# One table of instruction order exchanged for another, and the unread keys left unturned, in a fused attention and gated-MLP kernel

## The chip, the cores and the metric

The kernel runs on one core of a Trainium2 chip. The metric is device time in microseconds (us) of one execution; several executions are timed and their median is quoted. A profile is one execution recorded by the hardware profiler; its times count from the first instruction of the span.

## The reference

```python
B, H, S, D = 4, 8, 768, 48
for t in range(S):                                   # per batch and head
    state = alpha[t][:, None] * state + outer(k[t], v[t])
    y[t] = q[t] @ state
x = y.transpose(0, 2, 1, 3).reshape(3072, 384)
g = x @ w_gate                                       # 384 x 1536
out = ((g * sigmoid(g)) * (x @ w_val)) @ w_out       # 1536 x 384
```

All arrays are float32 (the weights arrive as float64 words and are reduced to single precision on the chip).

## The kernel before

**Tiling.** The recurrence is cut into 16 units: four batches of 768 tokens by four units of 192 tokens, each of three chunks of 64. Unit u of a batch is the last one where u is 3, 7, 11 or 15. Two units make one block of 384 rows for the MLP, so there are 8 blocks. The hidden width of 1536 is cut into 12 slices, and a step is one block and one slice: 96 steps, numbered in the order in which the program takes them (blocks 0 and 1 are taken in halves of 7 and 5 slices, the others whole).

**One step s** is a chain of words. `g` and `v` are nine matmuls each on TensorE (a value and its rounding remainder make three products per K tile), `sl` is SiLU on ScalarE, `h` the product with `v` on VectorE, `hh` the rounded copy on ScalarE, `hl` the remainder on VectorE or GpSimd, `o` nine matmuls into three accumulators. There is one PSUM bank for `g` (gps) and one for `v` (vps), so the next `v` waits for `h` of the step before, and the next `g` for its `sl`.

**One unit u.** `La`, `Lk`, `Lq` and `V` load alpha, keys, queries and values from SyncE (SP); the first four units are widened (`pa`, `pk`, `pq`) and turned by TensorE (`Ta`, `Tk`, `Tq`, evacuated by `ea`, `ek`, `cq`), the others are turned by VectorE (`tr`, `tk`, `tq`). `G` and `f` are the backward and forward scans, 1.8 us each on VectorE; `mk` and `q` multiply keys and queries by them, `qc` copies half of the queries. The keys are turned once more into the tile K: for the first four units by TensorE (`K`, copied by `kc`), for the others by VectorE (`kr`, lines 529 to 543: sixteen transposes a unit, each over all three chunks). `S` or a burst `Z` (from unit 4 on: outputs of unit u-1, scores and carried state of unit u in one run of small matmuls) use them; `ma` masks the scores, `ad` adds the carried state, `yh` and `yl` split the outputs, `xr` moves them by DMA (line 745) into the rows of xT that `g` and `v` read. The state that the last unit of a batch would carry past its third chunk is not computed (line 578), so its third chunk of K is not read.

**Weights.** `wl` loads a group, `w..v0` to `w..v2` cut it to single precision, `w..a` rounds it, `w..p` takes the remainder. `wr`/`wc` and `Lc`/`ck` load weights and alpha again for a range check, `fl` sums the verdicts (lines 828 to 839), `ot`/`os` take and store the outputs, `pl` loads a stored partial sum.

**Order.** Nothing schedules the program at build time but the table `ORDER` (line 44): each entry is an engine's letter (t TensorE, v VectorE, s ScalarE, g GpSimd, y SP) and a word, with the numbers of PSUM banks after an @. Each engine runs its words strictly in the order of the table; between engines only data and buffers order them. All loads and all `xr` are issued by SP, in order. The DMAs of the built program use eight semaphores in turn.

Of the kernel before, what the change touches and what calls it, by code (L numbers as in the profile page):

```python
# [49 lines left out]
t:Y0@36 s:yh0.0 y:La3 t:Ta2@20 s:pa3 s:ea2 y:Lk2 y:V1.0 s:w1a s:yh0.1 g:w1p y:Lq2 y:V1.3 y:V1.5 y:V1.2 v:w3v2 v:de1  # L50
t:S1@71 t:C1.0@2 s:ad1.0 v:yl0.0 v:ma1.2 t:Ta3@15 t:C1.1@4 s:ad1.1 t:C1.2@0 y:wl4 s:w4v0 s:ad1.2 g:pq2 g:pk2 g:vc1
v:ma1.1 v:yl0.1 v:ma1.0 t:Y1@64 s:yh1.0 v:w2v2 v:w2a s:yh1.1 t:R0.1@0 t:R0.2@3 t:Tq2@72 s:x0.2 s:x0.1 s:cq2 v:G2
v:yl1.0 v:yl1.1 t:R1.1@6 s:x1.1 v:w4v1 v:w4v2 t:Tk2@74 v:mk2 v:f2 v:q2 y:Lk3 s:pk3 t:R1.0@0 t:R0.0@6 y:V2.4 s:x0.0
s:x1.0 t:R1.2@7 s:x1.2 t:K2.0@2 s:kc2.0 g:w2p y:wl5 s:w5v0 y:V2.2 y:V2.0 y:Lq3 g:pq3 s:w4a t:Tk3@34 t:K2.1@7 s:kc2.1
t:g0 s:sl0 y:V3.1 y:V2.1 y:wl7 y:V2.3 y:V2.5 v:de2 g:vc2 g:lm0 y:V3.2 y:wl8 y:wl6 y:V3.3 y:V3.0 v:w5v1 s:ea3 v:G3
t:S2@20 s:qc2 v:ma2.2 v:mk3 v:ma2.0 v:lm1 y:wl11 y:wl9 y:V3.4 y:V3.5 s:w3a g:w3p g:w4p v:ma2.1 t:C2.0@7 t:K2.2@1
s:kc2.2 s:ad2.0 t:g1 t:v0 t:C2.1@3 v:h0 s:ad2.1 s:sl1 t:K3.0@7 s:kc3.0 t:Tq3@03 t:C2.2@1 s:ad2.2 s:cq3 s:hh0 s:w6v0
v:f3 t:v1 t:K3.1@7 t:g2 v:w5v2 g:hl0 v:h1 v:q3 v:de3 v:w6v1 s:hh1 s:kc3.1 s:sl2 t:Y2@20 s:yh2.0 v:hl1 v:w6v2 t:C3.0@4
t:S3@67 s:w5a g:w5p t:v2 s:ad3.0 t:C3.1@1 s:yh2.1 v:ma3.2 v:w8v0 v:yl2.0 s:w6a g:w6p t:o0 t:o1 v:ma3.1 v:yl2.1 y:wl12
y:La4 y:V4.5 y:wl10 s:w7v0 s:qc3 v:h2 v:ma3.0 y:xr2.0 y:xr2.1 v:w7v1 v:w7v2 v:w8v1 s:w9v0 s:ad3.1 s:vc3 t:g3 v:w8v2  # L60
v:w9v1 y:Lk4 y:wl13 y:xr2.2 t:Y3@20 s:sl3 s:w7a s:hh2 v:hl2 v:w7p s:w8a v:w8p s:yh3.0 s:yh3.1 t:v3 v:h3 s:w10v0 v:w9v2
s:hh3 v:hl3 t:g4 v:w10v1 s:sl4 s:w9a g:w9p t:o2 t:v4 v:yl3.1 v:yl3.0 v:h4 s:hh4 g:hl4 t:g5 v:w10v2 v:w10a s:w11v0
s:sl5 s:w12v0 t:v5 t:o3 v:w11v1 v:w10p t:g6 s:sl6 v:w12v1 v:w11v2 s:w11a v:h5 g:w11p s:hh5 t:o4 g:hl5 v:w12v2 y:xr3.0
y:xr3.1 y:xr3.2 y:wl16 y:V4.1 y:wl14 t:v6 v:tk4 v:h6 s:hh6 g:hl6 t:g7 v:tr4 v:G4 s:sl7 s:w13v0 s:w12a y:Lq4 v:mk4
# [1101 lines left out]
```

## Time and profile before

| what | value |
|---|---|
| timed runs | 550.12 us median (550.12, 547.42, 550.28) |
| profiled execution | span 548.1 us; its own device time is not listed beside the span |
| TensorE busy (PE) | 528.0 us, 96% of the span |
| VectorE busy (DVE) | 400.5 us, 73% |
| ScalarE busy (ACT) | 249.4 us, 45% |
| GpSimd busy (POOL) | 151.2 us, 28% |
| granted TensorE clock | 0.999 mean |
| DMA moved | 77.61 MB, 142 GB/s mean |

The busy time of an engine is the union of its instructions. SPq is the queue of SP, which only issues. An arrow in square brackets names what ended the idle time before an instruction. Matmul ends are modelled and overlap the next start, so the length of a run of matmuls is read from start to start.

### The profile page before, as it was taken

How to read it: one execution, taken by the hardware profiler on the slowest of the kernel's cores; microseconds unless marked ns; L12 is line 12 of the kernel's file. 1: busy time of each engine (PE TensorE's matmuls, PEld its weight loads, DVE VectorE, ACT ScalarE, POOL GpSimd, SP SyncE). 2: the span in 40 equal slices, each digit the busy share in tenths (PEclk: the TensorE clock that was granted, in tenths of full speed). 3: DMA queues.
4: the chain of work that ended last, by engine and by line, in shares of the span. 5: the costliest groups of instructions: out<-in, count | busy, mean ns of one | idle time of the engine just before them, and what ended most of it. 6: DMA issues, size and time to landing. Idle time of an engine off the chain costs nothing.

```text
span 548.1 us, 13557 instructions
## 1 busy us (share of the span) xinstructions
PE 528.0 (96%) x5350; PEld 513.7 (94%) x5350; DVE 400.5 (73%) x755; ACT 249.4 (45%) x578; POOL 151.2 (28%) x149
## 2 busy tenths in 40 slices
...
GB/s 243 256 263 292 146 173 249 107 139 174 85 187 151 141 106 185 157 120 73 169 76 101 203 158 112 76 136 129 184 153 73 90 50 158 135 58 104 155 50 47
DMA packets 96195, 77.61 MB, mean 142 GB/s; under 512 B 33280, under 2 KB 93056, under 8 KB 96128
## 3 DMA queue, kind: packets, MB, share of 16 engines
...
## 4 chain that ended last, share of the span: by engine, by line
PE 66%; DVE 3%; DMA 2%; SPq 1%; issue 1%; ACT 0%; POOL 0%; DVEq 0%; POOLq 0%
PE v L760 20%; PE ops L793 20%; PE g L760 20%; PE c L680 2%; PE s L565 1%; DMA L<-in_q_dram 1%; PE c L584 1%; PE y L658 1%; PE y L659 1%; DMA xT<-X 1%; SPq L745 1%; DMA V<-in_v_dram 1%; DVE h L772 0%; DVE V L629 0%; DVE K L540 0%
## 5 line engine op out<-in xcount | busy, mean ns | idle before, releaser
L760 PE MATMUL v<-xT,w 128*128 128x384 f32 x864 | 167.3, 337 | 0.6 <-DMA xT<-X 0.6
L760 PE MATMUL g<-xT,w 128*128 128x384 f32 x864 | 166.6, 336 | 0.6 <-ACT h L768 0.4
L793 PE MATMUL ops<-w,hh 128*128 128x384 f32 x576 | 158.5, 336 | 0.0
L760 PEld LDWEIGHTS v<-xT,w 128*128 128x128 f32 x864 | 150.5, 188 | 2.2 <-issue 0.9
L760 PEld LDWEIGHTS g<-xT,w 128*128 128x128 f32 x864 | 150.7, 188 | 1.8 <-ACT h L768 0.9
L781 POOL TENSOR_TENSOR hl<-h,hh 128x384 fp32r<-128x384 f32 x65 | 69.8, 1075 | 285.5 <-ACT hh L776 271.8
L772 DVE TENSOR_TENSOR h<-h,v 128x384 f32<-128x384 f32 x96 | 53.0, 552 | 89.9 <-PE v L760 61.6
L793 PEld LDWEIGHTS ops<-w,hh 128*128 128x128 f32 x576 | 105.5, 188 | 0.3
L768 ACT ACTIVATE h<-g 128x384 f32<-128x384 f32 x96 | 47.1, 490 | 119.6 <-PE g L760 101.0
L776 ACT CAST hh<-h 128x384 fp32r<-128x384 f32 x96 | 49.1, 511 | 112.0 <-DVE h L772 77.4
L793 PE MATMUL ops<-w,hl 128*128 128x384 f32 x288 | 96.8, 336 | 0.0
L540 DVE STREAM_TRANSPOSE K<-Gs 32x192 f32<-32x192 f32 x192 | 71.1, 370 | 3.3
L793 PEld LDWEIGHTS ops<-w,hl 128*128 128x128 f32 x288 | 54.0, 188 | 0.0
L347 POOL TENSOR_TENSOR w<-t,w 128x768 fp32r<-128x768 f32 (+1 forms) x15 | 27.5, 1842 | 34.4 <-ACT w L343 25.3
L781 DVE TENSOR_TENSOR hl<-h,hh 128x384 fp32r<-128x384 f32 x31 | 18.4, 594 | 22.8 <-ACT hh L776 22.7
L481 DVE TENSOR_TENSOR_SCAN AT<-AT,back 128x771 f32<-128x771 f32 x16 | 29.2, 1824 | 0.6
L606 DVE TENSOR_TENSOR X<-s,mask 64x384 f32<-64x384 f32 (+1 forms) x48 | 26.3, 551 | 3.8 <-PE s L565 3.1
L472 DVE TENSOR_TENSOR_SCAN Gs<-AT,inj 128x772 f32<-128x772 f32 x16 | 28.5, 1780 | 0.5 <-ACT AT L866 0.3
L497 POOL TENSOR_TENSOR X<-trq,AT 112x768 f32<-112x768 f32 x11 | 18.7, 1703 | 32.1 <-DMA xT<-X 11.0
L320 ACT ACTIVATE wc<-wc,wbias 128x384 f32<-128x384 f32 x36 | 23.3, 648 | 1.2
L629 DVE TENSOR_TENSOR V<-c,V 48x96 f32<-48x96 f32 x84 | 21.4, 255 | 2.8 <-ACT V L627 0.5
L893 POOL TENSOR_TENSOR Gs<-trk,Gs 128x768 f32<-128x768 f32 x9 | 15.3, 1700 | 26.0 <-DVE Gs L472 22.2
(120 smaller groups left out, 525.8 us busy)
## 6 DMA issues: line engine op xcount, KB each, us to landing
...
```

Of the source, the lines that this page charges most:

```text
L320: nc.scalar.activation(dev, dev, AF.Relu, bias=wbias, scale=-1.0, accum_out=wviol[:, 0, i : i + 1])
L347: eng.tensor_tensor(out=lo, in0=src, in1=hi.bitcast(F32), op=ALU.subtract)
L472: nc.vector.tensor_tensor_scan(*(x.rearrange("p g t -> p (g t)")[:, ::-1] for x in (Gs, AT, inj)), 0.0, op0=ALU.mult, op1=ALU.add)
L481: nc.vector.tensor_tensor_scan(Af, Af, back[:, 1 : n + 1], back[:, 0:1], op0=ALU.mult, op1=ALU.add)
L540: nc.vector.transpose(out=bass.AP(k0.tensor, k0.offset, [k0.ap[0], (G * 2 * D, NU), (2 * D, GF), (1, 32)]), in_=Kg[j * BO + x : j * BO + x ...
L606: nc.vector.tensor_tensor(out=X[r, z, f * GF : (f + 1) * GF, :].rearrange("r g (c t) -> r g c t", c=NU), in0=sps[f][r].rearrange("r g (c t ...
L760: nc.tensor.matmul(pt, wsp[kind, f][a][:, kt * P : (kt + 1) * P], xT[blk][:, b_, kt, :], start=(n == 0), stop=(n == 3 * KT - 1),)
L768: nc.scalar.activation(h, acc.pop(("g", blk, f)), AF.Silu)
L772: nc.vector.tensor_tensor(out=h, in0=h, in1=acc.pop(("v", blk, f)), op=ALU.mult)
L776: nc.scalar.copy(out=hh, in_=acc["h", blk, f])
L781: eng.tensor_tensor(out=hl, in0=acc.pop(("h", blk, f)), in1=hh.bitcast(F32), op=ALU.subtract)
L793: nc.tensor.matmul(ops[blk][i], h[b_][:, i * P : (i + 1) * P], wsp["o", f][a], start=(first and n == 0), stop=(last and n == 2),)
```

## The change

Two things are exchanged. The table `ORDER` is a different permutation of the same words: the order on each engine, the engine of some words (below) and most PSUM banks of the attention's early matmuls differ. And the third chunk of K is not turned where it is not read: `K3.2` and `kc3.2` (four TensorE transposes, two ScalarE copies) are dropped, and `kr` of units 7, 11 and 15 turns two chunks of three (48 VectorE transposes, 128 elements a row in place of 192).

Words by engine, before and after: `hl` GpSimd 65 to 61, VectorE 31 to 35; `q` GpSimd 11 to 8, VectorE 5 to 8; `qc` GpSimd 7 to 5, ScalarE 9 to 6, VectorE 0 to 5; `pq` GpSimd 3 to 0, ScalarE 1 to 3, VectorE 0 to 1; `pa` VectorE 1 to 0, ScalarE 3 to 4; weight rounding `w..a` ScalarE 18 to 15, VectorE 2 to 0, GpSimd 0 to 5; `ot` ScalarE 15 to 14, VectorE 15 to 16.

```diff
@@ ORDER: first and last lines of either table
-s:first y:La0 s:pa0 t:Ta0@23 s:ea0 y:wl0 y:Lq0 s:pq0 v:w0v0 v:w0v1 v:w0v2 v:G0 v:f0 t:Tq0@03 v:q0 y:La1 s:pa1 t:Ta1@72
-s:w0a v:w0p y:Lk1 s:pk1 y:Lk0 s:pk0 y:wl1 s:w1v0 t:Tk1@14 y:Lq1 t:Tk0@05 g:pq1 y:V0.2 y:V0.3 y:V0.1 v:w1v1 v:mk0 s:ea1
...
-s:hh92 s:wc24 v:hl92 s:sl94 t:v94 v:h94 t:o91 t:g93 y:Lc9 y:Lc13 s:sl93 t:v93 t:o92 v:h93 s:hh94 s:ck13 s:ck9 v:fl
-s:hh93 g:hl94 g:hl93 t:v95 t:g95 s:sl95 t:o93 t:o94 v:h95 s:hh95 v:hl95 t:o95 t:cp@2 v:ot95.0 y:os95.0 v:ot95.1
-s:ot95.2 y:os95.1 s:oz0 y:oz1 v:fg
+s:first y:La0 s:pa0 y:wl0 y:Lq0 y:La1 t:Ta0@65 v:w0v0 v:w0v1 y:Lk1 s:ea0 v:pq0 v:w0v2 s:pa1 t:Tq0@13 s:pk1 t:Ta1@42
+y:Lk0 v:G0 s:pk0 g:w0a t:Tk1@70 t:Tk0@56 y:V0.0 v:f0 v:q0 s:ek1 v:mk0 s:ea1 y:La2 y:V0.2 g:w0p y:Lq1 y:V1.3 y:V0.1
...
+v:h94 g:hl92 t:g93 t:o91 s:hh94 s:sl93 t:o92 t:v93 v:h93 t:g95 t:v95 s:hh93 s:wc24 v:hl93 s:sl95 s:wc33 t:o93 v:hl94
+v:h95 v:fl t:o94 s:hh95 v:hl95 t:o95 s:ot95.1 s:ot95.2 s:oz0 v:ot95.0 y:os95.0 t:cp@6 y:os95.1 y:oz1 v:fg
@@ k_rows
         k_tile(u)
-        Kg = state[u]["Gs"][:, :, 1:].rearrange("r g (c t) -> r c g t", c=NU)
+        nc_ = NU - last_of_batch(u)
+        Kg = state[u]["Gs"][:, :, 1:].rearrange("r g (c t) -> r c g t", c=NU)[:, 0:nc_]
...
-                    out=bass.AP(k0.tensor, k0.offset, [k0.ap[0], (G * 2 * D, NU), (2 * D, GF), (1, 32)]),
+                    out=bass.AP(k0.tensor, k0.offset, [k0.ap[0], (G * 2 * D, nc_), (2 * D, GF), (1, 32)]),
```

**VectorE at the start.** The first eleven rows from the cutting of the first weight group (t0, raw0) on; Gs0 is the backward scan of unit 0, AT the forward one, pt0_2 the turned queries and pt0_1 the turned keys of unit 0. Before:

```order
L175 SCALAR_TENSOR_TENSOR t0_154<-raw0_150,t0_154 128x384
L178 SCALAR_TENSOR_TENSOR t0_154<-raw0_150,t0_154 128x384
L472 SCALAR_TENSOR_TENSOR Gs0_158<-AT_85,inj_74 128x772
L478 RECIPROCAL back_88<-Gs0_158 128x4
L481 SCALAR_TENSOR_TENSOR AT_85<-AT_85,back_88 128x771
L482 MEMSET AT_85 128x3
L495 TENSOR_TENSOR X0_102<-pt0_2_0_163,AT_85 112x128x3
L495 TENSOR_TENSOR X0_102<-pt0_2_1_167,AT_85 112x128x3
L347 TENSOR_TENSOR w0_183<-t0_154,w0_183 128x384
L164 SCALAR_TENSOR_TENSOR t1_192<-raw1_190,t1_192 128x384
L890 TENSOR_TENSOR Gs0_158<-pt0_1_0_203,Gs0_158 128x4x32x3
```

and in the change:

```order
L174 SCALAR_TENSOR_TENSOR t0_152<-raw0_140,t0_152 128x384
L406 COPY wide_82<-Le_73 128x12x48
L177 SCALAR_TENSOR_TENSOR t0_152<-raw0_140,t0_152 128x384
L471 SCALAR_TENSOR_TENSOR Gs0_179<-AT_85,inj_74 128x772
L477 RECIPROCAL back_88<-Gs0_179 128x4
L480 SCALAR_TENSOR_TENSOR AT_85<-AT_85,back_88 128x771
L481 MEMSET AT_85 128x3
L494 TENSOR_TENSOR X0_102<-pt0_2_0_161,AT_85 112x128x3
L494 TENSOR_TENSOR X0_102<-pt0_2_1_165,AT_85 112x128x3
L890 TENSOR_TENSOR Gs0_179<-pt0_1_0_192,Gs0_179 128x4x32x3
```

The widening of the first queries (`pq0`, the COPY) has come from ScalarE to stand between the last two cuts; the remainder `w0p` and the cut `w1v1` have left the place ahead of `mk0` (the last row).

**TensorE at the first product**, from the last repacking of outputs (xp) on; kps2 are `K2` words, pt3_1 is `Tk3`, g0_0 the first `g`. Before:

```order
L731 MATMUL xp1_2_613<-Y1_552,sel1_122 128x384
L522 MATMUL kps2_0_617<-ident_90,Gs2_578 64x112 x4
L419 MATMUL pt3_1_0_636<-ident_90,wide_82 128x128 x3
L419 MATMUL pt3_1_1_640<-ident_90,wide_82 128x128 x3
L522 MATMUL kps2_1_644<-ident_90,Gs2_578 64x112 x4
L760 MATMUL g0_0_651<-xT0_547,w0_183 128x384 x9
```

and in the change:

```order
L731 MATMUL xp1_1_607<-Y1_554,sel0_121 128x384 x2
L521 MATMUL kps2_2_620<-ident_90,Gs2_565 64x112 x4
L521 MATMUL kps2_0_625<-ident_90,Gs2_565 64x112 x4
L760 MATMUL g0_0_634<-xT0_547,w0_182 128x384 x9
L418 MATMUL pt3_1_0_648<-ident_90,wide_82 128x128 x3
L418 MATMUL pt3_1_1_652<-ident_90,wide_82 128x128 x3
```

`Tk3` has moved from ahead of the first `g` to behind it.

**VectorE ahead of burst Z10**; trq11 is `tq11` (it reads the queries that `Lq11` loads), RECIPROCAL, L481 and MEMSET are `f11`, SE is `ad9.2`, h3_8 is `h44`, whose PSUM bank Z10 takes over. Before:

```order
L772 TENSOR_TENSOR h3_7_3751<-h3_7_3751,v3_7_3753 128x384
L399 STREAM_TRANSPOSE trq11_3791<-L0_71 128x4x6x32
L629 TENSOR_TENSOR SE_108<-c0_9_3480,V1_81 48x96 x2
L629 TENSOR_TENSOR SE_108<-c1_9_3481,V1_81 48x96 x2
L478 RECIPROCAL back_88<-Gs11_3708 128x4
L481 SCALAR_TENSOR_TENSOR AT_85<-AT_85,back_88 128x771
L482 MEMSET AT_85 128x3
L772 TENSOR_TENSOR h3_8_3725<-h3_8_3725,v3_8_3812 128x384
```

and in the change:

```order
L772 TENSOR_TENSOR h3_7_3791<-h3_7_3791,v3_7_3746 128x384
L477 RECIPROCAL back_88<-Gs11_3730 128x4
L480 SCALAR_TENSOR_TENSOR AT_85<-AT_85,back_88 128x771
L481 MEMSET AT_85 128x3
L772 TENSOR_TENSOR h3_8_3759<-h3_8_3759,v3_8_3808 128x384
L398 STREAM_TRANSPOSE trq11_3928<-L0_71 128x4x6x32
```

`tq11` has moved behind `h44`, and `ad9.2` ahead of `h43`.

## Rows read from the trace of the kernel before

**Rows 1.** The page's head: the span.

```profile
span 548.1 us, 13557 instructions
```

**Rows 2.** Stretches of the span, busy us (instructions) of each engine, PE clock, DMA.

```profile
0.00:36.51 36.51, 25.55 (x446) 21.43 (x447) 33.16 (x52) 28.46 (x66) 20.13 (x38) 1.00 0.88 244
36.51:130.00 93.49, 93.41 (x900) 89.91 (x898) 90.20 (x136) 54.07 (x106) 37.42 (x28) 1.00 0.67 186
130.00:360.00 230.00, 226.93 (x2468) 222.35 (x2467) 194.51 (x392) 76.17 (x190) 66.10 (x58) 1.00 0.54 135
```

**Rows 3.** TensorE's waits from 120 us on: us in total, times, longest.

```profile
PE y L658 <- DVE h L772: 1.8, 1, 1.8
PE v L760 <- DMA xT<-X: 0.6, 1, 0.6
PE g L760 <- ACT h L768: 0.4, 1, 0.4
...
PE c L584 <- issue: 1.0, 1, 1.0
```

**Rows 4.** Timeline of VectorE before burst Z10: start, duration, group.

```profile
274.02 1.61 DVE L399 STREAM_TRANSPOSE trq<-L 128x768 f32<-128x768 f32 x1 [2.02 <-DMA L<-in_q_dram]
...
278.74 0.55 DVE L772 TENSOR_TENSOR h<-h,v 128x384 f32<-128x384 f32 x1
```

**Rows 5.** Timelines of TensorE (v19) and VectorE (h19) near 145 us.

```profile
144.70 1.72 PE L760 MATMUL v<-xT,w 128*128 128x384 f32 x9
...
148.65 0.55 DVE L772 TENSOR_TENSOR h<-h,v 128x384 f32<-128x384 f32 x1
```

**Rows 6.** The start: ScalarE's pq0 and pa1; VectorE's w0v2, w0p, mk0.

```profile
7.71 1.38 ACT L407 COPY wide<-Le 128x576 f32<-128x576 f32 x2 [0.53 <-DMA Le<-in_q_dram]
6.66 0.90 DVE L178 SCALAR_TENSOR_TENSOR t<-raw,t 128x384 uint32<-128x384 uint32 x1
12.32 0.54 DVE L347 TENSOR_TENSOR w<-t,w 128x384 fp32r<-128x384 f32 x1
13.25 1.02 DVE L890 TENSOR_TENSOR Gs<-pt,Gs 128x384 f32<-128x384 f32 x2
```

**Rows 7.** Groups by form, VectorE then GpSimd: busy us, mean ns.

```profile
L407 DVE COPY wide<-L 128x576 f32<-128x576 f32 x1 | 0.8, 761 | 0.0
L781 DVE TENSOR_TENSOR hl<-h,hh 128x384 fp32r<-128x384 f32 x31 | 18.4, 594 | 22.8 <-ACT hh L776 22.7
L343 DVE CAST w<-t 128x768 fp32r<-128x768 f32 x1 | 1.3, 1261 | 0.0
L347 DVE TENSOR_TENSOR w<-t,w 128x768 fp32r<-128x768 f32 x4 | 3.7, 950 | 0.0
L540 DVE STREAM_TRANSPOSE K<-Gs 32x192 f32<-32x192 f32 x192 | 71.1, 370 | 3.3
L374 POOL CAST sel<-ident 48x48 fp32r<-48x48 f32 x4 | 4.0, 1008 | 0.2
```

**Rows 8.** Timeline at the first product: TensorE's Tk3, K2.1, g0; ScalarE's last copies of xT.

```profile
35.54 0.82 PE L419 MATMUL pt<-ident,wide 128*128 128x128 f32 x6
36.19 0.55 PE L522 MATMUL kps<-ident,Gs 112*64 112x112 f32 x4
36.51 1.84 PE L760 MATMUL g<-xT,w 128*128 128x384 f32 x9
34.50 1.29 ACT L735 CAST xT<-xp 128x384 fp32r<-128x384 f32 x3 [0.32 <-PE xp L731]
```

**Rows 9.** Timeline of TensorE at K3.2 and the product behind it.

```profile
88.36 0.55 PE L522 MATMUL kps<-ident,Gs 112*64 112x112 f32 x4
88.67 1.84 PE L760 MATMUL v<-xT,w 128*128 128x384 f32 x9
```

**Rows 10.** Timeline of VectorE at the end: the first verdict, and hl95.

```profile
534.18 0.18 DVE L834 TENSOR_REDUCE vsw<-wviol 128x1 f32<-128x36 f32 x1
540.48 0.56 DVE L781 TENSOR_TENSOR hl<-h,hh 128x384 fp32r<-128x384 f32 x1 [1.02 <-ACT hh L776]
```

More of the change, by code (lines that the diff above doesn't have):

```diff
@@ L50 @@
[L50 to L64, printed above, removed]
@@ L75 @@
-y:os13.2 y:pl18.2 y:wr3 y:V5.7 y:V5.5 y:pl18.1 g:qc5 s:hh17 g:w19p g:hl17 v:f6 t:o16 t:g19 s:sl19 v:kr5.1 v:kr5.0
-t:Z5@12560 s:yh4.0 v:yl4.0 v:ma5.0 v:ma5.1 g:w18p t:v18 g:mk6 v:kr6.0 v:ma5.2 v:h18 v:de5 s:yh4.1 s:yh4.2 v:ad5.0
-s:hh18 g:hl18 t:o17 t:g20 s:sl20 v:ad5.1 v:yl4.2 v:yl4.1 v:kr6.1 t:v19 v:h19 t:o18 v:ot18.2 s:hh19 g:hl19 v:tq6
-v:ot18.1 v:ad5.2 t:g21 t:v20 v:h20 s:sl21 s:hh20 g:hl20 y:La7 y:V6.1 y:V6.2 y:V6.6 y:V6.3 y:V6.5 y:V6.4 y:V6.7 y:V6.0
-v:de6 y:xr4.0 y:xr4.1 y:xr4.2 g:q6 y:os18.1 y:wr8 v:kr6.3 v:kr6.2 y:pl18.0 t:g22 t:v21 t:Z6@21704 s:yh5.0 v:yl5.0
@@ new lines @@
+y:Lk0 v:G0 s:pk0 g:w0a t:Tk1@70 t:Tk0@56 y:V0.0 v:f0 v:q0 s:ek1 v:mk0 s:ea1 y:La2 y:V0.2 g:w0p y:Lq1 y:V1.3 y:V0.1
+y:V0.5 s:pa2 y:V1.5 t:K0.0@1 v:G1 s:pq1 s:kc0.0 y:V0.3 t:K0.1@0 t:K0.2@7 t:C0.0@3 t:Tq1@61 s:kc0.1 g:qc0 s:kc0.2
+y:V0.4 v:mk1 t:K1.0@5 y:wl1 s:ad0.0 t:C0.1@3 s:cq1 y:wl2 s:ad0.1 v:f1 t:S0@74 v:ma0.0 v:ma0.2 v:ma0.1 y:wl3 t:C0.2@0
+y:V1.0 y:V1.1 t:K1.2@2 t:K1.1@1 g:vc0 y:V1.2 y:La3 g:q1 s:w1v0 s:ad0.2 s:kc1.0 v:de1 t:Y0@05 y:V1.4 v:w2v0 t:C1.0@6
+v:w1v1 s:qc1 s:kc1.1 t:S1@37 s:w3v0 s:yh0.0 s:ad1.0 s:yh0.1 v:w2v1 y:Lk2 v:w1v2 v:w3v1 s:pa3 s:kc1.2 t:Ta2@64 v:ma1.2
```

166 lines of the change are left out of this document (91 added, 75 removed).

## Prediction

> **What bounds the kernel now.** I read the span first, then busy time by stretch, then TensorE's waits, then the timelines around each wait. The span is 548.1 us [rows 1]. Up to the first MLP product, at 36.51 us, TensorE is busy for 25.55 us, so 10.96 are idle; from there to 130 us it idles 0.1 us, and from 130 to 360 us 3.1 [rows 2]. Its clock is granted in full in all three stretches, so idle time costs itself and no slower matmuls. From 120 us on TensorE waits for more than a third of a microsecond four times: 1.8 us for VectorE, 0.6 for rows of xT, 0.4 for ScalarE, and 1.0 where nothing that the profile shows is waited for [rows 3]. The kernel is thus bound by TensorE, and a new order of the same words can win three things only: the start, these 3.8 us, and the end. Meanwhile VectorE is busy for 33.16 of the first 36.51 us and 90.20 of the next 93.49 [rows 2]: where TensorE is late, VectorE's queue is the first suspect.
>
> Two of the waits are told by VectorE's rows. Ahead of burst Z10 `tq11` sat 2.02 us until the queries of `Lq11` had landed; `f11` and then `h44` were queued behind it, and Z10 needs the bank that `h44` frees at 278.74 plus 0.55 us [rows 4]. That is the 1.8: a late landing at the head of an in-order queue, not lack of time. The 0.4 is a backlog: `v19` ended at 146.42, `h19` began at 148.65 [rows 5], and through `hh19` and `hl19` the next SiLU, which needs the buffer of `h19`, held `g22`.
>
> The sum below is made against the 548.1 us of this execution; what lies around its span is not listed. The timed runs have a median of 550.12, and the lowest, 547.42, is below this span, so runs differ by as much as the waits that I count. I take the difference that comes out and set it off the median. The measurement can tell about 0.5% (2.75 us) from no change.
>
> **Keys not turned.** `K3.2` takes TensorE from 88.36 to 88.67 us [rows 9] between products that follow without idle time: -0.3. Its two copies are off the path. The 48 shorter VectorE transposes go from 0.37 us to about two thirds [rows 7], up to 5.9 us in all, spread over units 7, 11 and 15; none stands ahead of a wait that I count, so 0 on the path. If some other wait needed them it would gain; they can lose nothing.
>
> **The start.** Both orders issue the same six loads first, so the first queries land when they did. ScalarE waited for them until 7.71 us [rows 6]. `pq0` now sits on VectorE between `w0v1` and `w0v2`; `w0v2` used to start at 6.66 [rows 6], so VectorE stands idle for 1.05 us and then copies for 0.76 [rows 7]: +1.8 for G0 and all behind it. `w0p` and `w1v1` no longer stand ahead of `mk0`: from 12.32 to 13.25, -0.9 [rows 6]. So `mk0`, and with it the first K word on TensorE, comes 0.9 later. Later `pa2` (0.76, the same copy as [rows 7]) and `w2a` (about 0.6, an estimate: half of the 1.26 of the twice as wide rounding [rows 7]) are gone too, so by G2 VectorE has caught up. ScalarE's copies of xT ended at 35.79 before [rows 8]; its queue starts 0.9 later, and with `vc0`, `w1a` and `pk3` gone and `qc1`, `pk2` and `pq2` new it is as long as before within a few tenths. I place `g0` at 36.6, +0.1. But `Tk3` (35.54 to 36.19, 0.65 [rows 8]) has moved behind `g0`: at that time TensorE has done 0.65 less. The start costs +0.75; ends: -0.2 if ScalarE's queue has room, +1.9 if the whole delay of `pq0` arrives at `g0`. The loads `wl1` to `wl3` are issued behind ten more loads; `ma0` and `de1` cover that, since VectorE comes to the first cut only behind them. Without that cover it would be a wait like `tq11`'s, 2.0 [rows 4].
>
> **VectorE's backlog.** Ahead of `h20` the words on VectorE change so: `hl1`, `hl2`, `hl13` (0.59 each), `pa2` 0.76, `w0p` 0.54, `w2a` 0.6, `w10a` 1.26 and `w12p` 0.95 are gone, 5.9 us; `hl4` 0.59, `pq0` 0.76, `w5p` and `w11p` 0.95 each are new, 3.25 [rows 6, 7]. On TensorE the words ahead of `v20` are the same but for `K3.2`. So VectorE comes there 2.6 us earlier for the same work of TensorE, more than the 2.2 us by which `h19` was late [rows 5]: the 0.4 goes. What is late next there is GpSimd's `hl`, with 1 us to spare. At Z10 `tq11` is behind `h44`, so a late `Lq11` no longer holds the bank: the 1.8 goes too; behind `tq11` now stands `h45`, which TensorE needs only a burst and three products later. Together -2.2; ends -2.2 and 0, if VectorE's head waits on another landing.
>
> **Rows of xT.** In blocks 2 and 5 the rows of the odd unit arrive just ahead of their product, as in the wait of 0.6. In the change `xr5` is issued in one piece, where `Lq6` and a value load stood inside it, but `g24` comes one product (1.6 us) sooner after Z6; for `v60` the distance stays six products. I take 0; ends -0.6 and +1.6.
>
> **Unexplained wait.** 1.0 us inside the small matmuls of a burst [rows 3]. No word of the table removes it by a mechanism that I can see: 0; ends -1.0 and +1.0 (none, or a second one).
>
> **The end.** The eight verdict instructions (`fl`), none longer than 0.18 us by the first of them, move from ahead of `h95` to between `h95` and `hl95`: 1.4 us, while `hl95` had waited 1.02 for ScalarE [rows 10]. That is 0.4 late for a matmul that is not the first of `o95`: +0.1; ends 0 and +0.8 (behind the last range check as well).
>
> Sum: -0.3 + 0.75 - 2.2 + 0 + 0 + 0.1 = -1.65, a span of 546.4; from the median, **548.5**.
>
> **Against the change: GpSimd and VectorE.** Five roundings `w..a` move to GpSimd, three of them (w0, w1, w2) into the start. `w0v2` took 0.90 us [rows 6] while GpSimd was at its copies and roundings of constants, 1.0 us for a rounding of 48 x 48 elements [rows 7]. The price of a VectorE instruction held by one of the new roundings lies between 0 and those 1.0 us; I take 0, for the reason given with the third rival. The Trainium skill's page SBUF — State Buffer (Who interferes with whom) says that VectorE and GpSimd share one pair of ports under an exclusive lock, held for the whole instruction, which a copy on VectorE or one with two inputs in SBUF asks for. By that rule each rounding on GpSimd could hold VectorE for its full length; the long 0.90 agrees, but no row here tells a lock from a slow start.
>
> **Rivals.**
> - *The waits all go* (chance 0.27). With the start even (0), no wait for xT and no unexplained one: -0.3 - 2.2 - 0.6 - 1.0 = -4.1, **546.0**. For it: the lowest run of before, 547.42, lacks 2.7 us of the median, so runs with few waits exist. Against: `pq0` must wait for a landing that has not moved.
> - *Landings move to other places* (0.22). The 2.2 goes, but xT is 1.6 late at `g24`: about -0.05, **550.1**. For it: `tq8` and `q8` now stand right ahead of Z8, and `g24` has come closer. Against: `xr5` is no longer broken up.
> - *GpSimd holds VectorE* (0.09), slower. If each of the three roundings in the start holds VectorE for 1.0 us [rows 7], its lead of 2.6 is spent, `h19` stays late, and +0.75 - 0.3 + 3.0 = +3.45: **553.6**. It decides from a hold of about 0.8 us each. Against: four remainders of 768 elements with two inputs took VectorE 0.95 us each on the mean [rows 7], no more than twice the 0.54 of one of 384 [rows 6], though GpSimd was busy for 37.42 of the 93.49 us in which they lie [rows 2].
> - *The change does not do what it says*: the keys' third chunk is off the path of TensorE but for 0.3, so a failure there changes no number above.
>
> **How the numbers follow.** The forecast itself (547.0 to 550.0) has 0.42. Faster by over 0.5% (below 547.4): the first rival and a little of the forecast, 0.30. Slower (above 552.9): the third rival and a little of the second, 0.11. Within: 0.59. The range reaches from the first rival with half a microsecond more, 545.4, to 551.6, the second rival with a start at its upper end; the third rival is left out.
>
> **What would show it.** `pq0` on VectorE starting at 7.7 us and `mk0` near 14.2; `g0` at 36.6 with about 0.7 us more idle time before it; no wait of Z10 for `h44`, none of `g22` for a SiLU; `K3.2` absent; `hl95` a few tenths later against `o95`. Wrong would be a first product before 36 us or after 38, waits after 130 us of more than 4 us in sum, or a time below 545 or above 552.

## Result and profile after

The changed kernel took 542.88 us (median of 542.26, 542.77, 542.99 and 544.75); the kernel before, timed beside it, 549.93. The ratio is 0.9886, 95% interval 0.986 to 0.9912: about 7 us or 1.1% faster. The forecast was 548.5 with a range down to 545.4, so the sign was that of the sum and the size was missed. Two later timings gave 0.9898 (0.9852 to 0.9944) and 0.9900 (0.9882 to 0.9917).

The profiled execution is the one of 544.75 us; its span is 542.9. The stretches that answer to [rows 2]:

```profile
0.00:36.51 36.51, 25.16 (x441) 21.45 (x441) 29.80 (x50) 26.90 (x61) 23.32 (x40) 1.00 0.86 245
36.51:130.00 93.49, 92.74 (x898) 90.05 (x899) 88.68 (x133) 54.06 (x106) 43.88 (x34) 1.00 0.68 190
130.00:360.00 230.00, 229.85 (x2492) 226.73 (x2491) 195.90 (x401) 84.04 (x212) 57.06 (x51) 1.00 0.57 145
```

From 130 to 360 us TensorE idles 0.15 us in place of 3.1. These are all its waits of 0.2 us or more in the whole span; of those in [rows 3] none is left:

```profile
PE pt L418 <- ACT wide L406: 5.2, 1, 5.2
PE pt L418 <- DVE wide L406: 2.0, 1, 2.0
PE kps L521 <- DVE Gs L890: 1.7, 1, 1.7
PE y L659 <- issue: 1.1, 1, 1.1
PE y L680 <- issue: 0.8, 1, 0.8
PE s L565 <- issue: 0.8, 1, 0.8
PE g L760 <- ACT xT L735: 0.2, 1, 0.2
PE y L659 <- DVE X L606: 0.2, 1, 0.2
```

At Z10 VectorE's timeline, which answers to [rows 4], shows `h44` first, waiting for TensorE and no longer TensorE for it, and `tq11` behind it:

```profile
274.33 0.55 DVE L772 TENSOR_TENSOR h<-h,v 128x384 f32<-128x384 f32 x1 [0.75 <-PE v L760]
274.80 1.60 DVE L398 STREAM_TRANSPOSE trq<-L 128x768 f32<-128x768 f32 x1
```

The start on VectorE (`pq0`, `mk0`; [rows 6]), `g0` on TensorE ([rows 8]), and `hl95` at the end ([rows 10]):

```profile
8.15 0.49 DVE L406 COPY wide<-Le 128x576 f32<-128x576 f32 x1 [1.41 <-DMA Le<-in_q_dram]
13.84 1.01 DVE L890 TENSOR_TENSOR Gs<-pt,Gs 128x384 f32<-128x384 f32 x2
...
36.50 1.83 PE L760 MATMUL g<-xT,w 128*128 128x384 f32 x9 [0.19 <-ACT xT L735]
...
535.45 0.55 DVE L781 TENSOR_TENSOR hl<-h,hh 128x384 fp32r<-128x384 f32 x1
```

**Where the time went, by stretches.** The waits that are gone [rows 3] add up to 4 us; the timed medians differ by 7, the two profiled spans by 5.2. What is missing shows when both traces are cut at the same products. The table gives the time from the start of one product on TensorE to the start of another, at cuts ahead of which both orders have put the same products on TensorE. Several profiled executions are needed, since some stretches vary (the second of the changed kernel ran a part of its start at the lower clock, see the last section). *Keys* and *tq11* are experiments below that keep the order of before up to one word.

| stretch, us | before | keys | tq11 | changed | changed, 2nd | changed, 3rd |
|---|---|---|---|---|---|---|
| 0 to g5 | 68.01 | 67.91 | 68.68 | 69.14 | 69.92 | 66.92 |
| g5 to g17 | 52.16 | 52.15 | 52.10 | 51.74 | 51.74 | 51.74 |
| g17 to g22 | 31.32 | 31.36 | 31.25 | 29.67 | 29.67 | 29.74 |
| g22 to g42 | 110.33 | 109.96 | 110.12 | 109.53 | 109.60 | 109.60 |
| g42 to g50 (Z10, Z11) | 45.41 | 44.63 | 44.27 | 44.03 | 44.04 | 44.04 |
| g50 to g58 | 42.19 | 42.21 | 42.19 | 42.25 | 42.25 | 42.25 |
| g58 to g62 (v60) | 21.34 | 21.06 | 20.59 | 20.21 | 20.21 | 20.22 |
| g62 to g72 (Z14) | 49.75 | 49.10 | 49.47 | 48.75 | 48.76 | 48.74 |
| g72 to o95 | 120.76 | 120.76 | 120.75 | 120.76 | 120.75 | 120.76 |
| g5 to o95 | 473.24 | 471.23 | 470.74 | 466.94 | 467.04 | 467.09 |

Three things are to be seen. From `g5` on the gain is 4.1 to 4.3 us against *keys* and 6.3 against the profile of before. It sits in six stretches; the last 120 us are equal. And the three profiles with the old order (one each of before and of two kernels with a word out or moved) lie 2.5 us apart from `g5` on, the three of the changed kernel 0.15: there only the stretch up to `g5` varies.

### The profile page after: what moved, and what is told of

Read it like the earlier page. It is cut to its first block, busy times and chain, and to the rows that moved or that the text cites. A ratio compares the mean times of both kernels' runs of the same rounds, so it can differ in the third digit from the quotient of the medians.

```text
span 542.9 us, 13533 instructions
## 1 busy us (share of the span) xinstructions
PE 525.5 (97%) x5346; PEld 514.1 (95%) x5346; DVE 399.1 (74%) x766; ACT 245.1 (45%) x572; POOL 144.6 (27%) x142
## 4 chain that ended last, share of the span: by engine, by line
PE 92%; DMA 2%; DVE 2%; SPq 1%; ACT 1%; issue 1%; POOL 0%; POOLq 0%; ACTq 0%; DVEq 0%
PE g L760 27%; PE v L760 27%; PE ops L793 27%; PE s L565 2%; PE c L680 2%; PE pt L418 1%; PE y L659 1%; PE y L658 1%; DMA Le<-in_q_dram 1%; SPq L745 1%; PE c L584 1%; DVE X L606 1%; PE A L597 1%; PE y L680 1%; PE kps L521 1%
## 5 line engine op out<-in xcount | busy, mean ns | idle before, releaser
L793 PE MATMUL ops<-w,hh 128*128 128x384 f32 x576 | 160.5, 336 | 0.0
L781 POOL TENSOR_TENSOR hl<-h,hh 128x384 fp32r<-128x384 f32 x61 | 67.8, 1112 | 284.2 <-ACT hh L776 275.9
L540 DVE STREAM_TRANSPOSE K<-Gs 32x192 f32<-32x192 f32 (+1 forms) x192 | 67.9, 353 | 4.7 <-POOL Gs L893 1.2
L346 POOL TENSOR_TENSOR w<-t,w 128x768 fp32r<-128x768 f32 (+1 forms) x15 | 26.0, 1738 | 25.8 <-ACT w L342 25.3
L781 DVE TENSOR_TENSOR hl<-h,hh 128x384 fp32r<-128x384 f32 x35 | 20.5, 589 | 8.5 <-ACT hh L776 8.2
L893 POOL TENSOR_TENSOR Gs<-trk,Gs 128x768 f32<-128x768 f32 x9 | 15.2, 1691 | 22.4 <-DVE trk L398 11.5
L496 POOL TENSOR_TENSOR X<-trq,AT 112x768 f32<-112x768 f32 x8 | 13.6, 1696 | 27.0 <-DVE SE L629 12.5
```

What stands on the lines that cost most here:

```text
L346: eng.tensor_tensor(out=lo, in0=src, in1=hi.bitcast(F32), op=ALU.subtract)
L540: nc.vector.transpose(out=bass.AP(k0.tensor, k0.offset, [k0.ap[0], (G * 2 * D, nc_), (2 * D, GF), (1, 32)]), in_=Kg[j * BO + x : j * BO + ...
L781: eng.tensor_tensor(out=hl, in0=acc.pop(("h", blk, f)), in1=hh.bitcast(F32), op=ALU.subtract)
L793: nc.tensor.matmul(ops[blk][i], h[b_][:, i * P : (i + 1) * P], wsp["o", f][a], start=(first and n == 0), stop=(last and n == 2),)
```

## Experiments

Ratios are to the kernel before, run on the same chip, with 95% intervals. "Unread keys not turned" leaves `K3.2` and `kc3.2` out and shortens `kr` of units 7, 11 and 15, as the change does.

**1. The keys alone** (order of before).

```diff
-... g:hl8 t:K3.2@4 t:v9 v:h9 y:wl15 t:g10 s:kc3.2 s:sl10 ...
+... g:hl8 t:v9 v:h9 y:wl15 t:g10 s:sl10 ...
```

> The kernel before with only the unread keys left out (no K3.2, no kc3.2, 48 shorter VectorE transposes); the order is that of before. Theory (the order makes the gain): K3.2's 0.3 us and nothing else, 549.6 us. Rival (the keys make it): up to 5.9 us of VectorE's time is freed in units 7, 11 and 15, and if a wait needs it the time falls by 1 us or more, to 548.9 or below.

Measured: 548.39 us against 548.34, ratio 0.9983 (0.9956 to 1.001). From `g9` to `g12`, where `K3.2` stood, 14.58 us with it gone and 14.59 with it there. So not even the 0.3 came: the first matmuls of `v9` and `g10` now come late in its place. In the changed order the same stretch takes 14.14. So the keys alone bring nothing clear of noise, though the interval leaves room for some 2 us; from `g5` on the *tq11* kernel below, which turns them, was as short. What they are worth inside the changed order was not run.

**2. One word moved.** `tq11` behind `h44`. Here `tq11` reads the buffer after `Lk12` has taken it, so it turns keys of unit 12 in place of queries of unit 11; the instructions are the same.

```diff
-v:tq11 v:ad9.2 y:Lk12 ... v:f11 v:h44 v:kr10.1 t:Z10@12506
+v:ad9.2 y:Lk12 ... v:f11 v:h44 v:tq11 v:kr10.1 t:Z10@12506
```

> The kernel before with one word moved: tq11 stands behind h44 in place of ahead of ad9.2. Theory (a late landing at the head of VectorE's queue costs what the profile shows): Z10's wait of 1.8 us is gone and the time falls by 1.8 us, to 548.1. Rival (the wait belongs to the profiled execution, or another word is as late): no wait of Z10 for h44, or one of the next word in its place, and 549.9 us.

Measured: ratio 0.9995 (0.9964 to 1.0026). Z10's wait is gone, but it had been 1.0 us, not 1.8, in the *keys* execution, and 0.25 us of a new wait stands one burst later: the scores of Z11 wait for `q11` on GpSimd. Not because of the move: `tq11` had ended at 278.49, and the profile puts `q11`'s wait down to the `xr` transfers (xT<-X). `q11` starts 30.0 us behind `g42` in both kernels; TensorE, now earlier, meets it. `q11` in *keys*, then `tq11`, `q11` and Z11's scores in this kernel:

```profile
291.39 1.69 POOL L496 TENSOR_TENSOR X<-trq,AT 112x768 f32<-112x768 f32 x1 [3.72 <-DMA xT<-X]
```

```profile
276.88 1.61 DVE L399 STREAM_TRANSPOSE trq<-L 128x768 f32<-128x768 f32 x1
...
292.19 1.69 POOL L497 TENSOR_TENSOR X<-trq,AT 112x768 f32<-112x768 f32 x1 [4.81 <-DMA xT<-X]
...
293.94 0.75 PE L565 MATMUL s<-X,Gs 48*64 48x64 f32 x36 [0.25 <-POOL X L497]
```

The mechanism at Z10 was right; its price is what it costs at Z10 less what the next late word costs at Z11.

**3. Halves.** The two orders joined at `g17` (both: unread keys not turned).

```diff
+new_first: the changed table up to g17, then the rest in the order of before
+new_rest:  the table of before up to g17, then the rest in the changed order
```

> The changed order up to g17 (about 120 us), the order of before from there on; unread keys not turned. Theory (the two profiles, stretch by stretch): up to g17 the profile of the change is 0.7 us longer than that of before, so 550.6 us. Rival (the profile of the change is its slowest run, and the 2.6 us of waits without a releaser in its first 55 us are mostly this run's own): 1.8 us less, 548.8 us.

> The order of before up to g17 (about 120 us), the changed order from there on; unread keys not turned. Theory (the two profiles, stretch by stretch): from g17 on the profile of the change is 5.9 us shorter, so 543.7 us with K3.2's 0.3. Rival (part of the 7 us comes from the first 120 us): 545.5 us or more.

Measured: new first part 1.0011 (0.9987 to 1.0035), new rest 0.9958 (0.9929 to 0.9987). The halves don't add up to 0.9886. Part of the loss is at the joint: `g17` to `g22` took 30.83 and 30.73 us, each between 31.3 and 29.7. Cut where both orders have put the same words on TensorE, the stretch shows which half cures what:

| stretch, us (what is late there in the old order) | before | new first | new rest | changed | experiment 10 |
|---|---|---|---|---|---|
| g17 to o14 (`v16`) | 6.78 | 6.24 | 6.80 | 6.24 | 6.24 |
| o14 to v18 (Z5) | 12.92 | 12.98 | 13.00 | 12.51 | 14.08 |
| v18 to g22 (`v19`, `g22`) | 11.61 | 11.62 | 10.92 | 10.92 | 10.92 |

The new words of the first part cure `v16`, those of the rest `g22`. Between `o14` and `v18` the new rest has no late Z5, but TensorE waits for `h16` at `v17` instead (0.2 us of idle time), so that part needs both. And the first kernel met a wait of the old order that the profile of before does not show, 0.91 us at `o24` for a partial sum, which VectorE added after 2.65 us of idle time and 4.3 us after the load of the sum had been issued (the kernel of experiment 8, which has the old order there, waited 0.65 us at the same place):

```profile
187.42 0.44 PE L793 MATMUL ops<-w,hh 128*128 128x384 f32 x1 [0.91 <-DVE part L801]
```

**4. The changed kernel again, twice** (no edit).

> The changed kernel once more, with more executions and a second profile. Theory A (the waits without a releaser in the first profile, 0.8 us at 24.1, 1.1 at 30.2 and 0.8 at 54.8, are one execution's own): some of them are absent or of another size, the first product starts near 35.6 us as in the hybrid with the new first part, and the median is near 543 us. Theory B (they belong to the new order): all three come again within 0.2 us. Under both the ratio to before is 0.986 to 0.992.

> The changed kernel a third time, for a profile of a run at full clock. If what differs between its executions lies in the start (clock, landing of the first queries, waits without a releaser), g5 to o95 is 467.0 us again, within 0.1, and the first product lies between 35.0 and 36.5 us where the clock is granted in full; if it lies elsewhere, g5 to o95 differs by more than 0.3 us.

Measured: ratios as given above. `g5` to `o95` is the same within 0.15 us; `g0` came at 38.35 and 35.08 us, after 36.50. In the third, the two waits without a releaser in the burst of outputs are smaller and the one at 54.8 is gone:

```profile
PE pt L418 <- DVE wide L406: 1.2, 1, 1.2
PE y L659 <- issue: 0.8, 1, 0.8
PE y L680 <- issue: 0.3, 1, 0.3
```

So the start differs from one execution to the next by more than the +0.75 that I had summed for it.

**5. `pq0` behind G0** in the changed order. The move puts it behind `pk1`, with which it shares a buffer, so `Tk1` turns queries of unit 0 in place of keys of unit 1.

```diff
-s:ea0 v:pq0 v:w0v2 s:pa1 t:Tq0@13 s:pk1 t:Ta1@42 y:Lk0 v:G0 s:pk0
+s:ea0 v:w0v2 s:pa1 s:pk1 t:Ta1@42 y:Lk0 v:G0 v:pq0 t:Tq0@13 s:pk0
```

> The changed kernel with pq0 and Tq0 moved behind G0, so that VectorE no longer stands before w0v2 until the first queries have landed. Theory (the prediction's term of the start): VectorE was idle for 1.41 us there, so G0 and with it mk0 and the first K word come 1.0 to 1.5 us earlier, and g0 at about 35.0 us: 1 us less than the changed kernel. Rival (another queue ends last by then: ScalarE's copies or a landing of keys): mk0 earlier but g0 within 0.3 us of the changed kernel, no gain.

Measured: 0.9929 (0.9899 to 0.996). G0 starts at 7.50 us, but `pq0` then waits for ScalarE, and `mk0` comes at 14.17, later than 13.84:

```profile
10.26 0.46 DVE L406 COPY wide<-Le 128x576 f32<-128x576 f32 x1 [0.98 <-ACT wide L406]
...
14.17 1.02 DVE L890 TENSOR_TENSOR Gs<-pt,Gs 128x384 f32<-128x384 f32 x2
```

Neither came as written: `mk0` is later, not earlier, since another queue, ScalarE's, ends last; `g0` came at 35.80. This does not say what `pq0` in its new place costs. That is seen in *new_first*, where the queries had landed sooner: `pq0` at 7.36 and `mk0` at 13.20, as early as before [rows 6].

```profile
7.36 0.46 DVE L406 COPY wide<-Le 128x576 f32<-128x576 f32 x1 [0.70 <-ACT AT L866]
...
13.20 1.02 DVE L890 TENSOR_TENSOR Gs<-pt,Gs 128x384 f32<-128x384 f32 x2
```

**6. The old start with the rest new** (joined at `g5`).

```diff
+the table of before up to g5, then the rest in the changed order; unread keys not turned
```

> The order of before up to g5 (68 us), the changed order from there; unread keys not turned. Theory (the new start costs, the rest gains): g5 at 68.0 us in place of 68.4 to 69.1, and from g5 to the last product 467 to 468 us as in the changed kernel: 0.4 to 1.1 us less than the changed kernel, about 542.3. Rival (the new start pays later, since it leaves VectorE less work behind): from g5 on 1 us or more longer than in the changed kernel, above all from g17 to g22, and the time above the changed kernel's.

Measured: 544.38 us, 0.9922 (0.989 to 0.9954), beside 544.06 of the changed kernel on the same chip: no gain. From `g5` on 466.71 us, as in the changed kernel, with `g17` to `g22` at 29.67: that stretch needs the new order from `g5`, not the new start. So the rest came as expected and did not get longer for the old start, but the old start gained nothing. `g5` itself came at 72.21, since this execution ran a part of its start at the lower clock (last section).

**7. Three repairs to the order of before**, unread keys not turned.

```diff
-v:tq11 v:ad9.2 y:Lk12 ... v:h44        +v:ad9.2 ... v:h44 v:tq11 y:Lk12
-v:w10a s:w11v0 s:sl5                    +s:w10a s:w11v0 s:sl5
-v:hl1 ... v:hl2 ... v:w12p              +g:hl1 ... g:hl2 ... g:w12p
-y:V13.4 y:os47.0 y:xr11.0 y:xr11.1 ... y:V13.7 y:xr11.2
+y:xr11.0 y:xr11.1 ... y:xr11.2 y:V13.7 y:os47.0 y:V13.4
```

> The order of before, unread keys not turned, with three small repairs taken from the change: tq11 and then Lk12 behind h44; w10a from VectorE to ScalarE, w12p, hl1 and hl2 from VectorE to GpSimd in their places; the three loads ahead of xr11.2 put behind it. Theory (three late places make most of the gain, each by its own mechanism): against the order of before without unread keys, g17 to g22 falls by 0.5 to 1.6 us (31.36 to about 30.3), g42 to g50 by 0.4 to 0.9 (44.63 to about 44.0), g58 to g62 by 0.5 to 0.8 (21.06 to about 20.4): 2.2 us in all. Rival (the gain is spread over the whole order and no single place carries it): none of the three stretches falls by more than 0.3 us.

Measured: 1.0045 (1.0016 to 1.0075), slower. `g17` to `g22` stayed at 31.30; `g42` to `g50` was 44.89, since Z10's wait came back whole at Z11 (1.04 us for `q11`); `g58` to `g62` was 20.59, no better than in *tq11*, which has no repair there. And `g5` to `g12` grew from 33.37 to 34.40, for two reasons that the trace shows. A cut on VectorE had to wait for ScalarE, where `w10a` now stood ahead of it; and the two remainders `hl1` and `hl2` held VectorE from GpSimd. `de3` (two inputs in SBUF) beside `hl1`, and the same instruction in *keys*, where `hl1` is on VectorE:

```profile
72.12 0.96 DVE L163 SCALAR_TENSOR_TENSOR t<-raw,t 128x768 uint32<-128x768 uint32 x1 [1.79 <-ACT t L162]
...
49.62 1.53 DVE L635 SCALAR_TENSOR_TENSOR V<-SE,Gs 48x192 f32<-48x192 f32 x2
...
49.12 1.43 POOL L781 TENSOR_TENSOR hl<-h,hh 128x384 fp32r<-128x384 f32 x1 [0.24 <-ACT hh L776]
```

```profile
49.69 0.73 DVE L635 SCALAR_TENSOR_TENSOR V<-SE,Gs 48x192 f32<-48x192 f32 x2
```

Taking 0.55 us from VectorE cost it 0.80 us here.

**8. `w10a` to ScalarE, where it holds nobody up** (order of before, unread keys not turned).

```diff
-v:w10v2 v:w10a s:w11v0 s:sl5 s:w12v0
+v:w10v2 s:w11v0 s:sl5 s:w10a s:w12v0
```

> The order of before, unread keys not turned, with one word moved: the rounding w10a goes from VectorE (1.26 us, of which 0.79 held by a remainder on GpSimd) to ScalarE, behind w11v0 and sl5, where it can hold no cut of VectorE up. Theory (from 40 to 155 us VectorE is behind, and the waits of v16, Z5 and g22 are one backlog): 1.3 to 2.1 us less work ahead of h15 takes away v16's wait (0.45) and part of the others, g17 to g22 from 31.36 us to 30.9 or less. Rival (the waits come from the order of the words on VectorE, not from how many there are): g17 to g22 stays within 0.2 us of 31.36.

Measured: 1.0015 (0.9987 to 1.0044). `g17` to `g22` 31.25: within 0.2 us, so the rival holds. Less work on VectorE 30 us earlier does not shorten this stretch in the order of before.

**9. More work on VectorE** in the changed order.

```diff
-v:kr4.3 v:kr4.0 s:w15v0
+v:kr4.3 v:kr4.0 v:rr4.3 v:rr4.0 s:w15v0
```

> The changed kernel with 3.06 us of VectorE work added behind kr4.0 (kr4.3 and kr4.0, eight transposes, done twice; the result is the same). Theory (backlog): the changed order has at h15 a lead of no more than half a microsecond, so the old waits come back: g17 to g22 from 29.67 us to 31 or more. Rival (VectorE has room there): g17 to g22 within 0.3 us of 29.67.

Measured: 0.9987 (0.9967 to 1.0007). Of the 3.06 us added, 2.7 came back at once, at the next two products, and 0.38 in `g17` to `g22`: 3.04 from `g5` to `o95`. (The median rose by more, 547.25 us against 542.66 of the changed kernel on the same chip; this one profile does not show the rest.)

```profile
101.56 1.86 PE L760 MATMUL v<-xT,w 128*128 128x384 f32 x9 [0.79 <-DVE h L772]
104.55 0.61 PE L760 MATMUL g<-xT,w 128*128 128x384 f32 x2 [1.14 <-ACT h L768]
```

The stretch that I named did not carry it, so this does not show a lead at `h15`. It shows that VectorE has no room to spare near 100 us: what is put ahead of an `h` there costs TensorE its full length.

**10. Transposes behind the scan** in the changed order.

```diff
-t:o15 v:kr5.1 v:kr5.0 s:sl18 s:hh17 g:mk6 v:f6
+t:o15 s:sl18 s:hh17 g:mk6 v:f6 v:kr5.1 v:kr5.0
```

> The changed kernel with the transposes kr5.1 and kr5.0 behind the scan f6 in place of ahead of it, as in the order of before. Theory (the wait of 0.30 us in the middle of burst Z5, which the profile of before puts down to nothing, is for kr5.0): VectorE turns the keys 1.8 us later, Z5 waits in its middle again, g17 to g22 from 29.67 us to about 30.1. Rival (the wait has another cause): g17 to g22 within 0.1 us of 29.67.

Measured: 0.9933 (0.9915 to 0.9951). `g17` to `g22` went to 31.24 us: +1.57 where I had expected 0.4. That is as much as the two orders differ by, but not in the same places: all of it lies between `o14` and `v18`, 1.2 us more than the old order needs there, and the waits of `v16` and `g22` did not come back (table of experiment 3). Of this kernel, the scan `f6` and, on GpSimd, `mk6`:

```profile
131.00 2.82 DVE L480 TENSOR_TENSOR_SCAN AT<-AT,back 128x771 f32<-128x771 f32 x1
...
130.50 1.69 POOL L893 TENSOR_TENSOR Gs<-trk,Gs 128x768 f32<-128x768 f32 x1 [1.70 <-DVE Gs L471]
```

Of the changed kernel, the eight transposes `kr5.1`, `kr5.0`, the scan behind them, and `mk6`:

```profile
132.59 3.06 DVE L540 STREAM_TRANSPOSE K<-Gs 32x192 f32<-32x192 f32 x8
...
135.91 1.82 DVE L480 TENSOR_TENSOR_SCAN AT<-AT,back 128x771 f32<-128x771 f32 x1
...
132.20 1.69 POOL L893 TENSOR_TENSOR Gs<-trk,Gs 128x768 f32<-128x768 f32 x1 [1.71 <-DVE Gs L471]
```

Beside `mk6` the scan takes 2.82 us in place of 1.82; the transposes take 0.37 us each there, as everywhere (3.06 for eight). So the swap costs 1.0 us of VectorE's time in the changed order, and Z5 waits 0.62 us for the late `kr5.0`. The old order has the scan ahead of the transposes too and does not pay this: in *keys* no `mk` runs at that time, the scan takes its 1.82 us, and the remainder that GpSimd starts beside it takes 2.12 in place of 1.02:

```profile
134.02 1.82 DVE L480 TENSOR_TENSOR_SCAN AT<-AT,back 128x771 f32<-128x771 f32 x1
...
134.53 2.12 POOL L781 TENSOR_TENSOR hl<-h,hh 128x384 fp32r<-128x384 f32 x1 [0.56 <-ACT hh L776]
```

So this experiment gives the price of a swap, not the cause of the difference between the two orders. The Trainium skill's page SBUF — State Buffer (Who interferes with whom) says that a VectorE instruction with two inputs in SBUF contends with a GpSimd instruction that reads SBUF, and that one with a single input outside the two-port modes does not; the scan (1.0 us longer) and the transposes (no longer) agree.

**11. Three moves in the order of before**, no word on another engine, unread keys not turned.

```diff
-v:f6 t:o16 t:g19 s:sl19 v:kr5.1 v:kr5.0 t:Z5@12560
+t:o16 t:g19 s:sl19 v:kr5.1 v:kr5.0 v:f6 t:Z5@12560
-y:V13.4 y:os47.0 y:xr11.0 y:xr11.1 ... y:V13.7 y:xr11.2
+y:xr11.0 y:xr11.1 ... y:xr11.2 y:V13.4 y:V13.7 y:os47.0
-y:Lk15 y:os59.2 y:V14.6 g:q14 y:V14.2 y:V14.4
+y:V14.6 g:q14 y:V14.2 y:V14.4 y:Lk15 y:os59.2
```

> The order of before, unread keys not turned, with three moves and no word on another engine: f6 behind kr5.1 and kr5.0 (as in the change); the three other transfers that stood among xr11 behind xr11.2; Lk15 and os59.2 behind V14.4. Theory (single places in the order carry most of the gain from g5 on): against the same order without the moves, g17 to g22 falls from 31.3 us to about 29.9, g58 to g62 from 21.06 to about 20.4, and g62 to g72 from 49.1 to about 48.7 because Z14 finds its last values landed: 2.4 us in all, a median near 546. Rival (the swap costs 1.5 us in the changed order only, where VectorE has other work there): g17 to g22 stays above 31.0 us.

Measured: 1.005 (1.0025 to 1.0075), slower. `g17` to `g22` grew to 32.79. The stall in the middle of Z5 is gone, but here `f6` falls beside the end of `w19p` and the whole of `mk6` on GpSimd, and `yl4.0`, which frees the bank of `v18`, is queued behind it:

```profile
141.37 3.36 DVE L480 TENSOR_TENSOR_SCAN AT<-AT,back 128x771 f32<-128x771 f32 x1
144.77 0.55 DVE L709 TENSOR_TENSOR X<-y,X 112x384 fp32r<-112x384 f32 x1
...
141.43 1.67 POOL L893 TENSOR_TENSOR Gs<-trk,Gs 128x768 f32<-128x768 f32 x1
...
145.38 0.79 PE L760 MATMUL v<-xT,w 128*128 128x384 f32 x3 [1.82 <-DVE X L709]
```

In the changed order VectorE comes 1.1 us earlier to `h16` (counted from `g17`), the cuts `w19v1` and `w19v2` stand behind `h17`, and `o16` stands between Z5 and `v18`. Which of these makes the swap pay there was not tried; without them it costs. `g58` to `g62` was 20.62. Z14 still waited 0.59 us, though the last values of unit 14 had landed 6 us before: the wait is not for them.

**12. Loads ahead of Z14** in the changed order, in two variants.

```diff
-y:xr12.1 y:xr12.2 v:q14
+fetch_busy:  y:xr12.1 y:xr12.2 y:wr1 y:Lc3 y:Lk15 v:q14
+fetch_busy2: y:xr12.1 y:xr12.2 y:wr1 y:Lk15 v:q14
```

> The changed kernel with three loads (wr1, Lc3, Lk15) issued ahead of burst Z14, behind xr12.2, where SP issues nothing in the changed order. All waits of TensorE without a releaser in the profiles so far stand at the records 449, 705, 1473 and 8641 of TensorE's matmuls and weight loads, that is at whole multiples of 256 from each other; 8641 lies in Z14, where the order of before waited 0.34 to 1.02 us with DMAs busy and the changed order never did, with its DMAs idle for 3.5 us ahead. Theory (the next piece of the instruction stream comes late when the DMAs are busy): with the loads there, the wait comes back at record 8641, 0.2 to 1.2 us, and nowhere else from 60 us on. Rival (the DMAs have no part in it): no wait in Z14, as in the changed kernel.

> As fetch_busy, but with wr1 and then the four transfers of Lk15 alone, since Lc3 there waited for its buffer until Z14 was over and the DMAs were busy for 0.13 to 0.37 of the time only. Theory (late instruction supply under DMA load): DMA share above 0.5 in the 3 us ahead of record 8641 and a wait of 0.2 to 1.2 us there. Rival: no wait at record 8641 with that share.

Measured: 0.9849 (0.9811 to 0.9888) and 0.9901 (0.9882 to 0.9919); `g62` to `g72` 48.76 in both, no wait in Z14. In the second the DMAs were busy (last but one column) right ahead of record 8641, which fell at 391.24 us, yet later than in *keys*, whose two rows follow:

```profile
386.93:389.93 3.00, 3.00 (x56) 2.68 (x57) 2.85 (x8) 1.20 (x4) 0.00 (x0) 1.00 0.37 113
389.93:391.93 2.00, 1.86 (x140) 1.73 (x129) 1.70 (x5) 1.85 (x4) 0.00 (x0) 1.00 0.93 252
```

```profile
385.00:390.00 5.00, 5.00 (x35) 4.75 (x36) 2.90 (x8) 1.06 (x3) 3.00 (x3) 1.00 0.70 169
390.00:393.00 3.00, 2.66 (x155) 2.46 (x155) 1.86 (x6) 2.07 (x6) 0.56 (x1) 1.00 0.41 90
```

In the 3 us up to the record the share was 0.76, as the expectation asked, and there was no wait: the rival holds as far as these go. Whether traffic some 4 to 8 us ahead matters was not tried, so the cause of the size stays open.

## Why the prediction was wrong

**What failed first: the size of a stall was read from the list of waits.** The prediction put 0.4 on `g22` and held that a new order "can win three things only: the start, these 3.8 us, and the end". The stretch of that 0.4 gained 1.65 us (31.32 to 29.67). Of this, 0.69 lie between `v18` and `g22`; 0.54 lie at `v16`, ahead of which the trace has 0.06 us of idle time, and 0.41 around Z5, with 0.10. A matmul's end is modelled past the next start, so such lateness counts as busy and is in no list of waits. The terms set at nothing, for xT and for the wait without a releaser, were worth 0.4 to 1.1 and 0.4 to 1.0 (below).

**What failed next: VectorE's backlog.** The 0.4 did go, but not by the step that foretold it. The eight words that leave VectorE and the four that join it ("2.6 us earlier") all stand ahead of `h15`, so *new first* has all of them and *new rest* has none. In *new first* `g22` waits as before:

```profile
PE g L760 <- ACT h L768: 0.4, 1, 0.4
```

In *new rest* it does not (the nine matmuls of `g22`, with no idle time ahead):

```profile
151.04 1.72 PE L760 MATMUL g<-xT,w 128*128 128x384 f32 x9
```

So this wait went by the order of the words behind `h16`; the new words ahead of it, these twelve among them, cure `v16` and no more by themselves. Which words behind `h16` do it is not shown; it is not `f6` alone, since putting it back ahead of the transposes (experiment 10) did not bring the wait back.

What GpSimd holds was not in the count either: beside a rounding remainder a cut of 0.55 us took 1.75 (53.13 us, *keys*); in the changed kernel it stands elsewhere and takes 0.55:

```profile
53.13 1.75 DVE L171 TENSOR_SCALAR t<-raw 128x768 uint32<-128x768 uint32 x1
```

```profile
58.57 0.55 DVE L171 TENSOR_SCALAR t<-raw 128x768 uint32<-128x768 uint32 x1
```

**Step by step.**
- *Keys, -0.3:* 0.0 in the order of before (experiment 1). The shorter transposes take 0.303 us, not two thirds of 0.37.
- *The start, +0.75:* the term "VectorE stands idle for 1.05 us" holds only where the first queries land late (8.15 us); with `pq0` at 7.36, `mk0` is not later at all. What was mis-sized is the way from `mk0` to `g0`, 22.4 us in the forecast (36.6 less 14.2): it took 23.3 to 23.5 us in the five profiles with the old first part at full clock, and in six with the new one 20.6 to 20.8 us and, on top, 0.5 to 1.9 us of waits for nothing that the profile shows (last section). That `g0` came at 36.50 in the first profile, right beside the forecast, is luck: 1.9 us of it are such waits. On the mean the six reach `g5` at 67.4 us (66.1 to 69.1), the five at 68.3 (67.9 to 68.9): -0.9, against the forecast's sign, though less than the spread. The part on `Tk3` was right: `g0` to `g5` is 0.5 us longer in the third profile (31.84 against 31.34).
- *Backlog and Z10, -2.2:* both waits went, that of Z10 by the mechanism given (experiment 2), that of `g22` not by it. Measured: -1.65 at `g17` to `g22`, and -0.6 (against *keys*) to -1.4 at `g42` to `g50`.
- *xT rows, 0:* -0.4 to -1.1 at `g58` to `g62`, steady at 20.2 in every execution of the new rest. The end "-0.6" was the likelier one; I chose the middle. Which of the moves does it is not shown: the old order took 20.59 and 20.62 with the three transfers put behind `xr11.2` (experiments 7 and 11), and 20.59 to 21.38 in five kernels without.
- *Unexplained wait, 0:* -0.4 to -1.0 at `g62` to `g72`. It went, although no word removes it "by a mechanism that I can see".
- *The end, +0.1:* 0.00 (`g72` to `o95` equal).
- *The base:* "I take the difference and set it off the median" of three runs, 550.12. Over more runs the median of before was 548.3 to 548.5, and its profiled execution was a long one from `g5` on (473.24 us; 471.23 and 470.74 in the two kernels that keep its order). So single waits in that profile were larger than usual, while the sum of all lateness, listed or not, was larger than the list.

Sum of the stretches: -0.9 for the start, and against *keys* -0.4, -1.65, -0.4, -0.6, -0.85 and -0.35 from `g5` on, about -5.1; against the first profile of before -7. The medians of the timings differ by 4.5 to 7.1.

**The rivals.** *The waits all go* came nearest (546.0) and was still 3 us high, by what lay outside the list and by the base. *Landings move* did not happen. *GpSimd holds VectorE* is a real mechanism with the wrong place: the new roundings on GpSimd held no instruction for 0.8 us (the scan G0 took 1.75 beside `w0a`), but holds of 0.8 to 1.5 us do occur: for `de3` beside `hl1` (experiment 7), the cut above, and `f6` beside `mk6` (experiments 10 and 11). The changed order has a little less of them: between 36 and 160 us VectorE's instructions took 1.2 us in all beyond the usual length of their form before (1.5 in *keys*), 0.6 us in the change (each one's time less the lower quartile of its form and shape, where it is over by more than 0.12). That is too little for the 4.2 us from `g5` on. It can be GpSimd that is held as well (experiment 10, *keys*).
